# Four steps of the first batches moved in an attention-and-MoE kernel: k1's transposes, a copy of a1, the permutation of v3, the load of k4

## The chip, the core and the metric

The kernel runs on one core of one Trainium2 chip. The core has five engines with queues of their own, each worked off in order: TensorE (PE in the profile; its weight loads are PEld), VectorE (DVE), ScalarE (ACT), GpSimd (POOL) and SyncE (SP). Sixteen DMA engines serve all of them. The metric is the device time of one execution in microseconds (us). Before the change it is 252.37 us, the median of seven runs (249.28 to 253.69).

## What is computed

```python
def _attn_ref(q, k, v, p):
    def sm_attn(qq, kk, vv):
        s = scale * np.matmul(qq, kk.transpose(0, 1, 3, 2))
        s = s - np.max(s, axis=-1, keepdims=True)
        a = np.exp(s)
        a = a / (np.sum(a, axis=-1, keepdims=True) + 1e-09)
        return np.matmul(a, vv)
    p_packed = sm_attn(p, k, v)
    out = sm_attn(q, p_packed, p_packed)
    return out.astype(np.float32)

def _moe_ref(x, w_in, w_out):
    h = x @ w_in
    g = h * np.cos(h)
    return (g @ w_out).astype(np.float32)
```

q, k and v are 8 batches x 8 heads x 576 rows x 64 in float32, p is 8 x 8 x 32 x 64. In a first attention 32 packed queries per head look at all 576 keys; in the second one the 576 queries look at the 32 packed results. The heads of a row are put side by side (4608 rows of 512), go through w_in (512 x 2048), are multiplied by their own cosine, and go through w_out (2048 x 512).

## The kernel before

The kernel works batch by batch, in bf16. The loads of q, k and v (`load`) are DMAs from GpSimd's queue that cast to bf16 on the way. For each batch b there follow, by the names of the code:

- kT and qT: k and q with the head's 64 numbers on the partitions. They are made either by 24 TensorE transposes in three groups, each copied out of PSUM (`pe_T`), or by one transposing DMA on SP's queue (`xbar`).
- `s1`: scores of p against k, 16 matmuls, two exponentials on ScalarE into a1 with the sums beside them. a1T is a1 transposed, by TensorE (`a1_pe`, `a1_one`) or by a DMA on SP (`a1_xbar`).
- `permute_v`: one copy that puts v's heads side by side (vp). `pp`: 24 matmuls of vp with a1T, which give the packed results, copied to ppT.
- `ppw`: the packed results times a quarter of w_in (PPW, four quarters, n = 0 to 3). So w_in is applied to 32 packed rows per head, and the second attention is applied after it.
- `s2`, `sums2`, `normalise`: scores of q against the packed results, exponentials (a2u), their sums by a matmul with blocks of ones, a logarithm and an exponential on ScalarE for the inverse, and two products on VectorE (a2n).
- `h_mm`, once for each of 16 chunks fc of 128 hidden columns: four matmuls of PPW and a2n into a psA tile, the cosine on ScalarE, the product with the cosine on VectorE (gT).
- `out_gen`, used as `fill(n)`: the next n matmuls of gT and w_out for an earlier batch, with the copy to osb and the store on SP's queue at the end of each row block. They are spread between the other work of TensorE.

The order of the work is written out by hand; each engine runs its instructions in the order of the code. A "front" is the part from one batch's chunks to the next (table load for the exponential, `s2`, `sums2`, `normalise` and the next batch's `s1`), a "slot" (`slot`) the 16 chunks, with steps hung in after given chunks (the hooks) and fills in between. The first front, for batch 0, is lines 349 to 403 and slot 0 is lines 404 to 418; front 1 is lines 442 to 460, slot 1 lines 461 to 463, front 2 lines 465 to 499, slot 2 line 500. From batch 3 on, lines 502 to 535 repeat one pattern. `warm(n)` are matmuls on zeros in the first front.

What the change and the steps of the prediction touch:

- psA: three PSUM tiles of two banks, used in turn by nearly every step of TensorE; a chunk's tile comes free when its gT product is done. ot: two banks for the fills.
- bf: the loaded tiles. k has two buffers, q and v one each. The load of the next q waits until the transpose of the last one has read it; the load of the next v until the permutation has read it. vp has two buffers.
- GpSimd's queue holds, in the order of the code, all loads of q, k, v and the weights, the permutations of v from batch 1 on, `dup_p` for batches 2 to 7, and two joint copies per batch (line 267: the last 64 rows of gT, which two batches share).
- Lines 452 to 456 of front 1: transpose of q2 on SP, permutation of v2, load of v3, permutation of v3, load of q3. The load of k4 hangs in slot 1 after chunk 8 (line 462).
- SP's queue in fronts 1 and 2: transpose of q2 (line 452), stores, transpose of k3 (slot 1, after chunk 12), stores, transposes of q3, a1 of batch 3 and k4 (lines 483 to 486).
- Line 496: GpSimd copies one element of kT of batch 4 ("gate"), so that the loads of v4, q4 and k5 behind it are held until that transpose has landed.
- `pp(3)` is hung in slot 2 after chunk 7, `pp(4)` in slot 3 after chunk 5 (line 535).

Of the kernel before, what the change touches and what calls it, by code (L numbers as in the profile page):

```python
# [15 lines left out]
def kernel(  # L16
# [16 lines left out]
    C = 6  # L33
    TP = S // C
# [20 lines left out]
    V, ACT, G = nc.vector, nc.scalar, nc.gpsimd  # L55
# [17 lines left out]
    def copy(eng, out, in_):  # L73
        if eng is ACT:
            ACT.copy(out=out, in_=in_)  # L75
        else:
            eng.tensor_copy(out=out, in_=in_)  # L77

    def psa(dt=FP32):
        return A.tile([128, 2, 512 if dt == FP32 else 1024], dt, name="psA", tag="A")  # L80

    def load(n, b):
        bf[n, b] = bf_pool.tile([TP, H, C * D], BF16, name=n + "bf", tag=n + "bf", bufs=2 if n == "k" else 1)
        G.dma_start(out=bf[n, b], in_=srcs[n][b].rearrange("h (p c) d -> p h (c d)", c=C))

    def permute_v(b, eng=G):
        vp[b] = vp_pool.tile([TP, C, H * D], BF16, name="vp", tag="vp")
        copy(eng, vp[b].rearrange("p c (h d) -> p c h d", h=H),
             bf["v", b].rearrange("p h (c d) -> p c h d", c=C))
# [5 lines left out]
    def pe_T(n, b, engs=(V, V, V), groups=(0, 1, 2), own=False):  # L95
        if 0 in groups:
            xT[n, b] = att_pool.tile([128, H * 3, TP], BF16, name=n + "T", tag=n + "T", bufs=2 if n == "k" else 1)
        t = xT[n, b]
        flat = bf[n, b].rearrange("p h x -> p (h x)")
        for i in groups:  # L100
            ps = bank(BF16) if own else psa(BF16)[:, 0, :]
            for j in range(8):
                o = 8 * i + j
                nc.tensor.transpose(ps[:, j * TP:(j + 1) * TP], flat[:, o * 128:(o + 1) * 128],  # L104
                                    ident[0:TP, 0:TP])
            copy(engs[i], t[:, 8 * i:8 * i + 8].rearrange("p a x -> p (a x)"),
                 ps[:, 0:8 * TP])

    def bank(dt=FP32):
        return O.tile([128, 512 if dt == FP32 else 1024], dt, name="ot", tag="ot")  # L110

    def pack_p(b0, b1, flat=None):
        ng = 2 * (b1 - b0)
        if flat is None:
            flat = psa(BF16).rearrange("p a x -> p (a x)")
        for g in range(ng):
            nc.tensor.transpose(flat[:, g * 128:(g + 1) * 128],
                                p_bf[:, 2 * b0 + g].rearrange("p t d -> p (t d)"), ident)
        V.tensor_copy(out=P2[:, b0:b1].rearrange("p b h n -> p (b h n)"), in_=flat[:, 0:ng * 128])
# [14 lines left out]
    def s1(b, later=False):  # L134
        ps = scores(P2[:, b], xT["k", b])
        sm = sums1[b] = small.tile([128, 2], FP32, name="sums1")

        def exps():
            for y in range(2):
                ACT.activation(  # L140
                    out=a1[b % 2][:, y, :, 0:TP].rearrange("p (e m) x -> p e m x", e=2),
                    in_=ps[y][:, :, 0:HS].rearrange("p e (m x) -> p e m x", m=3),
                    func=AF.Exp, scale=scale, accum_out=sm[:, y:y + 1])
        if later:
            return exps
        exps()

    def recips(b):
        r1[b] = small.tile([128, 2], FP32, name="r1")
        rs1[b] = small.tile([128, 2], FP32, name="rs1")  # L150
        V.reciprocal(r1[b], sums1[b])
        V.tensor_scalar(out=rs1[b], in0=r1[b], scalar1=scale, scalar2=None, op0=ALU.mult)
# [16 lines left out]
    def a1_one(b):  # L169
        t = a1T[b] = att_pool.tile([128, 2, C, 128], BF16, name="a1T", tag="a1T")  # L170
        ps = psa(BF16)
        for y in range(2):
            for c in range(C):
                nc.tensor.transpose(ps[0:TP, y, c * 128:(c + 1) * 128], a1[b % 2][:, y, c, 0:TP], ident)
        for y in range(2):
            copy(V, t[0:TP, y].rearrange("p c x -> p (c x)"), ps[0:TP, y, 0:C * 128])

    def pp(b, own=False, engs=(V, ACT)):
        ps = bank() if own else psa()[:, 0, :]
        for hp in range(4):  # L180
            for j in range(C):
                c = 2 * (j % 3) + j // 3
                nc.tensor.matmul(ps[:, hp * 64:(hp + 1) * 64], vp[b][:, c, hp * 128:(hp + 1) * 128],  # L183
                                 a1T[b][0:TP, :, j, 32 * hp:32 * hp + 32], start=(j == 0), stop=(j == C - 1))
        pv = ps[:, 0:256].rearrange("p (a y x) -> p a y x", a=4, y=2)
        t = ppT[b % 2].rearrange("p (a y) x -> p a y x", y=2)
        for y in range(2):
            r = slice(64 * y, 64 * y + 64)
            copy(engs[0], t[r, :, y, :], pv[r, :, y, :])
        for y in range(2):  # L190
            r = slice(64 * y, 64 * y + 64)
            z = slice(64 - 64 * y, 128 - 64 * y)
            copy(engs[1], t[z, :, y, :], pv[r, :, y, :])
# [27 lines left out]
    def s2(b):  # L221
        a2u[b] = att_pool.tile([128, 2, S], BF16, name="a2u", tag="a2u")
        ps = scores(ppT[b % 2], xT["q", b])
        for y in range(2):
            ACT.activation(out=a2u[b][:, y].rearrange("p (e x) -> p e x", e=2),  # L225
                           in_=ps[y][:, :, 0:HS], func=AF.Exp, scale=rs1[b][:, y:y + 1])

    def sums2(b, y):
        if b not in lns:
            lns[b] = att_pool.tile([128, 2, S], FP32, name="lns", tag="lns")  # L230
        ps = psa()
        for e in range(2):
            nc.tensor.matmul(ps[:, e, 0:HS], ones_blk, a2u[b][:, y, e * HS:(e + 1) * HS],  # L233
                             start=True, stop=True)
        ACT.activation(out=lns[b][:, y].rearrange("p (e x) -> p e x", e=2),  # L235
                       in_=ps[:, :, 0:HS], func=AF.Ln)
# [89 lines left out]
    def fill(n):  # L326
        while n > 0 and filler[1] > 0:
            next(filler[0])
            filler[1] -= 1
            n -= 1  # L330
# [13 lines left out]
    def warm(n):  # L344
        wps = bank()
        for _ in range(n):
            nc.tensor.matmul(wps, wz[:, 0:128], wz, start=True, stop=True)  # L347
# [38 lines left out]
        load_w_out(n)  # L386
    G.dma_start(out=p_raw[:, 4:, :], in_=p_rows[:, 4:, :])
    s2(0)
    warm(3)
    sums2(0, 0)  # L390
    sums2(0, 1)
    pe_T("k", 1, (V, V, V))
    warm(2)
    s1_mm = s1(1, later=True)
    cut_ppw, rest_ppw = ppw(0, 0, V, own=True, later=True, cuts=((0, 256), (256, 512)))
    normalise(0)
    s1_mm()
    cut_ppw()
    a1_one(1)
    rest_ppw()  # L400
    load("k", 2)
    permute_v(1)
    load("v", 2)
    for fc in range(NFC):
        rest = h_mm(0, fc)
        if fc in (11, 12, 13):
            pe_T("q", 1, (V, ACT, V), (fc - 11,), own=True)
        rest()
        if fc in (1, 5, 8):
            ppw(0, 1 + fc // 4, (ACT, V), own=True)  # L410
        if fc == 3:
            recips(1)
        if fc == 10:
            pp(1, own=True, engs=(ACT, ACT))
        if fc == 13:
            set_filler(0)
        if fc >= 14:
            fill(2)

    def slot(s, hooks, keep=0, heavy={}):  # L420
        left = filler[1] - keep
        out_eng[:] = (ACT,) if s > 1 else (V, ACT)
        weight = [1 + heavy.get(fc, 0) for fc in range(NFC)]
        for fc in range(NFC):
            h_mm(s, fc)()
            quota = (left * sum(weight[:fc + 1])) // sum(weight) - (left + keep - filler[1])
            first = quota
            while hooks and hooks[0][0] == fc:
                if first == quota and fc in heavy:
                    first = quota // 2  # L430
                    fill(first)
                hooks.pop(0)[1]()
            fill(quota - first if first != quota else quota)

    def pw2(b, n=0, eng=None):
        ppw(b, n, eng)
        ppw(b, n + 1, eng)

    def tk(n, b, i):
        return lambda: pe_T(n, b, (V, V, V), (i,))  # L440
# [11 lines left out]
    xbar("q", 2)  # L452
    permute_v(2)
    load("v", 3)
    permute_v(3)
    load("q", 3)
    ppw(1, 1, V)
    normalise(1)
    ACT.preload_act_table_set(SIN_SET)
    fill(14)  # L460
    slot(1, [(3, lambda: pw2(1, 2, (ACT, V))), (5, tk("k", 2, 0)), (6, tk("k", 2, 1)),
             (7, tk("k", 2, 2)), (8, lambda: load("k", 4)), (9, lambda: pack_p(2, 5)),
             (11, lambda: pack_p(5, B)), (12, lambda: xbar("k", 3))], 4, {3: 3})

    ACT.preload_act_table_set(EXP_SET)
# [1 line left out]
    fill(1000)  # L467
    set_filler(1)
    s1(2)
    fill(5)  # L470
    a1_pe(2, (0,))
    fill(2)
# [24 lines left out]
    for n, b in (("v", 4), ("q", 4), ("k", 5)):  # L497
        load(n, b)
    fill(5)
    slot(2, [(7, lambda: pp(3, engs=(ACT, ACT))), (11, lambda: pw2(3))], 5, {11: 3})  # L500

    for s in range(3, B):
        nxt = s + 1 < B
# [66 lines left out]
```

## Time and profile before

| what | us |
|---|---|
| median of seven runs | 252.37 |
| the runs | 249.28 to 253.69 |
| the profiled execution's own time | 252.37 |
| its span, first to last instruction | 250.6 |
| TensorE matmul busy | 236.3 |
| VectorE / ScalarE / GpSimd busy | 167.3 / 167.0 / 57.4 |
| granted TensorE clock, mean | 0.999 |

The stretches of the first part, as busy microseconds of each engine and as the rate of the DMA engines:

| stretch (us) | PE | DVE | ACT | POOL | GB/s |
|---|---|---|---|---|---|
| 10 to 20 | 8.65 | 5.40 | 5.82 | 3.85 | 205 |
| 20 to 25 | 3.94 | 4.73 | 4.38 | 1.47 | 205 |
| 25 to 30 | 4.49 | 4.97 | 4.45 | 2.07 | 206 |
| 30 to 35 | 4.24 | 4.54 | 4.12 | 3.88 | 206 |
| 35 to 40 | 5.00 | 4.35 | 4.85 | 0.82 | 206 |
| 50 to 60 | 9.77 | 8.71 | 5.54 | 3.52 | 145 |
| 60 to 70 | 9.92 | 6.97 | 5.56 | 4.22 | 229 |
| 70 to 80 | 9.60 | 7.79 | 6.74 | 1.18 | 169 |
| 80 to 90 | 9.29 | 6.82 | 7.84 | 0.18 | 166 |
| 110 to 120 | 8.36 | 6.48 | 7.08 | 2.99 | 143 |

How to read the lines that follow. A line of the timeline has a start, a length, the engine, the line of the kernel, the operation, the tile that it writes, the tile that it reads, the shape and the count; square brackets give the idle time of the engine just ahead of it and what ended that. The chain of waits goes from what ended last back to what released it; it is shown in order of time, with a start and a length. A line of the waits names who waited, for what, the sum in us, how often and the longest. "To landing" is the time from a DMA's issue until its data had arrived.

### The profile page before, as it was taken

The page shows a single profiled execution, that of the slowest core. Times are in us where ns is not written, and L with a number is a line of the kernel's source. Part 1 is how long each engine was busy: PE and PEld are TensorE (multiplying, and loading weights), DVE is VectorE, ACT ScalarE, POOL GpSimd, SP SyncE. Part 2 cuts the span into 40 slices and gives each one's busy share as a digit, 9 for nine tenths or more (in the row PEclk, how much of TensorE's full clock was granted, in tenths as well). Part 3 has the DMA queues.
Part 4 walks back from the last instruction along what each step waited for, and adds up shares of the span by engine and source line. Part 5 has one row for each costly group of instructions (what it writes and reads, how often), then busy time and mean ns, then how long its engine had stood idle before and what let it go on. Part 6 is the DMA issues. An engine that isn't in the chain of part 4 may idle for free.

```text
span 250.6 us, 5070 instructions
## 1 busy us (share of the span) xinstructions
PE 236.3 (94%) x2038; PEld 131.3 (52%) x2038; DVE 167.3 (67%) x253; ACT 167.0 (67%) x278; POOL 57.4 (23%) x68
## 2 busy tenths in 40 slices
PE   8688899999999899979999999999999999999993
PEld 3454474566544554455546654565456554665452
DVE  2449997689668767676848666678766774876110
ACT  2358899746566787868867867887777684874000
POOL 8162543250430043103330405020500000000000
PEclk9999999999999999999999999999999999999999
DMA  6999999999999989996999996989391112202133
GB/s 90 202 205 205 205 206 228 199 163 137 239 175 166 179 148 214 155 190 131 193 195 220 161 220 141 186 160 207 80 167 42 42 44 67 61 15 66 44 86 84
DMA packets 63175, 37.09 MB, mean 148 GB/s; under 512 B 35792, under 2 KB 58576, under 8 KB 63152
## 3 DMA queue, kind: packets, MB, share of 16 engines
q0 software_dynamic: 23152, 18.75, 49.7%
q1 hardware_dynamic: 39840, 17.90, 35.6%
q8 instruction: 16, 0.26, 0.5%
q10 hardware_dynamic: 160, 0.13, 0.2%
q14 instruction: 7, 0.06, 0.1%
HBM read 37.22 MB, written 9.44 MB: 186 GB/s over the span
## 4 chain that ended last, share of the span: by engine, by line
PE 72%; DMA 17%; DVE 5%; ACT 2%; POOL 2%; issue 1%; DVEq 0%; POOLq 0%
PE ot L309 43%; PE psA L256 19%; DMA w_out_bf<-in_moe_w_out_dram 9%; DMA w_in_bf<-in_moe_w_in_dram 7%; DVE gT L263 3%; PE psA L207 3%; PE psA L183 2%; DMA a1T<-a 2%; PE psA L129 2%; ACT cosT L260 2%; PE ot L295 1%; PE psA L233 1%; DVE PPW L77 1%; ACT ppT L75 1%; DVE a2n L243 1%
## 5 line engine op out<-in xcount | busy, mean ns | idle before, releaser
L309 PE MATMUL ot<-w_out_bf,gT 128*128 128x512 bf16 x512 | 133.3, 379 | 0.1
L263 DVE TENSOR_TENSOR gT<-psA,cosT 128x576 bf16<-128x576 f32 x128 | 93.8, 756 | 28.9 <-ACT cosT L260 28.1
L260 ACT ACTIVATE cosT<-psA 128x576 bf16<-128x576 f32 x128 | 82.5, 652 | 27.8 <-PE psA L256 23.1
L256 PE MATMUL psA<-a2n,PPW 128*128 128x288 bf16 x512 | 83.5, 286 | 1.4 <-DVE PPW L77 0.4
L309 PEld LDWEIGHTS <-gT 128*128 128x128 bf16 x512 | 47.7, 98 | 43.3 <-issue 6.8
L256 PEld LDWEIGHTS <-PPW 128*128 128x128 bf16 x512 | 49.3, 98 | 34.5 <-issue 4.2
L77 DVE CAST PPW<-psA 128x1024 bf16<-128x1024 f32 (+1 forms) x23 | 26.9, 1175 | 11.6 <-PE psA L207 11.5
L77 DVE COPY osb<-ot 128x512 f32<-128x512 f32 (+1 forms) x24 | 16.3, 679 | 17.5 <-PE ot L309 13.9
L267 POOL COPY joint<-gT 128x512 bf16<-128x512 bf16 x16 | 9.9, 617 | 78.9 <-DVE gT L263 78.9
L77 POOL COPY vp<-vbf 96x3072 bf16<-96x3072 bf16 x7 | 19.3, 2751 | 14.3 <-DMA vbf<-in_v_dram 14.3
L75 ACT COPY osb<-ot 128x512 f32<-128x512 f32 (+1 forms) x13 | 7.3, 565 | 15.3 <-PE ot L309 10.6
L243 DVE SCALAR_TENSOR_TENSOR a2n<-a2u,r,lns 128x576 bf16<-128x576 bf16 x16 | 12.3, 813 | 7.3 <-ACT lns L241 7.3
L235 ACT ACTIVATE lns<-psA 128x576 f32<-128x576 f32 x16 | 10.2, 650 | 7.1 <-PE psA L233 6.5
L140 ACT ACTIVATE a<-psA 128x576 bf16<-128x576 f32 x16 | 10.3, 647 | 6.7 <-PE psA L129 6.7
L309 PE MATMUL ot<-w_out_bf,joint 128*128 128x512 bf16 x48 | 12.8, 379 | 0.0
L75 ACT CAST ppT<-psA 64x128 bf16<-64x128 f32 x24 | 6.2, 260 | 9.1 <-DVE ppT L77 6.0
L225 ACT ACTIVATE a2u<-psA,rs 128x576 bf16<-128x576 f32 x16 | 11.0, 737 | 1.4 <-PE psA L129 1.3
L207 PE MATMUL psA<-w_in_bf,ppT 64*32 64x512 bf16 x224 | 10.2, 381 | 0.0
L241 ACT ACTIVATE lns<-lns 128x576 f32<-128x576 f32 x16 | 10.0, 676 | 0.0
L347 PE MATMUL ot<-wz 128*128 128x512 bf16 x26 | 8.1, 447 | 1.2 <-DVE wz L359 1.2
L522 POOL COPY gate<-kT 1x1 bf16<-1x1 bf16 x3 | 0.5, 181 | 36.6 <-DMA kT<-kbf 36.6
L77 DVE COPY kT<-psA 128x768 bf16<-128x768 bf16 x8 | 4.2, 552 | 6.8 <-PE psA L104 6.6
(71 smaller groups left out, 155.9 us busy)
## 6 DMA issues: line engine op xcount, KB each, us to landing
kbf<-in_k_dram POOLq DMA_DIRECT2D x8, 576.0 KB, 12.9
vbf<-in_v_dram POOLq DMA_DIRECT2D x8, 576.0 KB, 8.6
qbf<-in_q_dram POOLq DMA_DIRECT2D x8, 576.0 KB, 10.1
out_dram<-osb SPq DMA_DIRECT2D x24, 192.0 KB, 3.1
out_dram<-osb SPq DMA_DIRECT2D x22, 128.0 KB, 2.4
w_in_bf<-in_moe_w_in_dram POOLq DMA_DIRECT2D x4, 512.0 KB, 17.1
w_out_bf<-in_moe_w_out_dram POOLq DMA_DIRECT2D x4, 512.0 KB, 21.4
out_dram<-osb SPq DMA_DIRECT2D x26, 64.0 KB, 2.1
```

What stands on the lines that cost most here:

```text
L75: ACT.copy(out=out, in_=in_)
L77: eng.tensor_copy(out=out, in_=in_)
L140: ACT.activation(out=a1[b % 2][:, y, :, 0:TP].rearrange("p (e m) x -> p e m x", e=2), in_=ps[y][:, :, 0:HS].rearrange("p e (m x) -> p e m ...
L207: nc.tensor.matmul(ps[y][32 * x:32 * x + 32, :], ppT[b % 2][r, 2 * x + y, :], w_in_bf[r, x, n * 512:(n + 1) * 512], start=True, stop=True)
L225: ACT.activation(out=a2u[b][:, y].rearrange("p (e x) -> p e x", e=2), in_=ps[y][:, :, 0:HS], func=AF.Exp, scale=rs1[b][:, y:y + 1])
L235: ACT.activation(out=lns[b][:, y].rearrange("p (e x) -> p e x", e=2), in_=ps[:, :, 0:HS], func=AF.Ln)
L241: ACT.activation(out=lns[b][:, y], in_=lns[b][:, y], func=AF.Exp, scale=-1.0)
L243: V.scalar_tensor_tensor(out=a2n[b][:, y], in0=a2u[b][:, y], scalar=r1[b][:, y:y + 1], in1=lns[b][:, y], op0=ALU.mult, op1=ALU.mult)
L256: nc.tensor.matmul(ps[:, e, 0:HS], PPW[b][:, y, fc * 128:(fc + 1) * 128], a2n[b][:, y, e * HS:(e + 1) * HS], start=(y == 0), stop=(y == 1))
L260: ACT.activation(out=csv, in_=ps[:, :, 0:HS], func=AF.Sin, bias=PI_HALF)
L263: V.tensor_tensor(out=gT[b][:, fc, :].rearrange("p (e x) -> p e x", e=2), in0=ps[:, :, 0:HS], in1=csv, op=ALU.mult)
L309: nc.tensor.matmul(pss[c], w, w_out_bf[:, fc, :], start=(fc == 0), stop=(fc == NFC - 1))
```

## The change

Four edits, all in the part up to slot 2:

1. In the first front the three groups of k1's transposes, which stood behind both sums of batch 0, are put ahead of, between and behind the two sums. The warm-up matmuls around them go from 3 and 2 to 1 and 3.
2. `a1_one(1)` copies the first half of a1T of batch 1 on VectorE as before and hands back the second copy, which ScalarE makes after chunk 0 of slot 0. The call moves behind `rest_ppw()`.
3. The permutation of v3 moves from GpSimd in front 1 to VectorE in slot 2, after chunk 4.
4. The load of k4 moves from slot 1 (after chunk 8) to front 2, behind `s1(2)`.

```diff
@@ a1_one @@
-        for y in range(2):
-            copy(V, t[0:TP, y].rearrange("p c x -> p (c x)"), ps[0:TP, y, 0:C * 128])
+        copies = [lambda eng, y=y: copy(eng, t[0:TP, y].rearrange("p c x -> p (c x)"), ps[0:TP, y, 0:C * 128])
+                  for y in range(2)]
+        copies[0](V)
+        return copies[1]
@@ first front @@
     s2(0)
+    warm(1)
+    for i in range(3):
+        pe_T("k", 1, (V, V, V), (i,))
+        if i < 2:
+            sums2(0, i)
     warm(3)
-    sums2(0, 0)
-    sums2(0, 1)
-    pe_T("k", 1, (V, V, V))
-    warm(2)
     s1_mm = s1(1, later=True)
...
     cut_ppw()
-    a1_one(1)
     rest_ppw()
+    rest_a1 = a1_one(1)
     load("k", 2)
@@ slot 0 @@
         rest()
+        if fc == 0:
+            rest_a1(ACT)
@@ front 1 and slot 1 @@
     load("v", 3)
-    permute_v(3)
     load("q", 3)
...
-             (7, tk("k", 2, 2)), (8, lambda: load("k", 4)), (9, lambda: pack_p(2, 5)),
+             (7, tk("k", 2, 2)), (9, lambda: pack_p(2, 5)),
@@ front 2 @@
     s1(2)
+    load("k", 4)
@@ slot 2 @@
-    slot(2, [(7, lambda: pp(3, engs=(ACT, ACT))), (11, lambda: pw2(3))], 5, {11: 3})
+    slot(2, [(4, lambda: permute_v(3, V)), (7, lambda: pp(3, engs=(ACT, ACT))), (11, lambda: pw2(3))], 5, {11: 3})
```

## The prediction

> **What bounds the kernel now.** I read the page's busy times first, then its chain of work that ended last, then TensorE's waits, and last the timelines of the four places that the edits touch.
>
> ```profile
> span 250.6 us, 5070 instructions
> PE 236.3 (94%) x2038; PEld 131.3 (52%) x2038; DVE 167.3 (67%) x253; ACT 167.0 (67%) x278; POOL 57.4 (23%) x68
> ```
>
> TensorE (PE) is idle for only 14.3 us of the span, so a reordering that leaves its work alone can win no more than part of that. The chain of waits says where the first stretch stands:
>
> ```profile
> 5.10 0.76 POOL w_in_bf L333
> 5.85 16.43 DMA w_in_bf<-in_moe_w_in_dram
> 22.57 21.75 DMA w_out_bf<-in_moe_w_out_dram
> 44.36 0.81 PE ot L309 x3
> ```
>
> Up to 44 us the end is set by loads that run back to back. The table of stretches gives 205 GB/s from 10 to 25 us and 206 from 25 to 40, so the stream has no hole to close. TensorE meets it three times: at the fourth projection in slot 0 (w_in's last quarter, 31.08 us), at the transposes of q1 (34.01), and at the first fill that needs w_out's last quarter (44.36). From 35 to 45 us it is busy 9.88 of 10 us. What TensorE waits for after that is in its own waits:
>
> ```profile
> PE psA L183 <- DVE gT L263: 1.6, 1, 1.6
> PE psA L183 <- DMA a1T<-a: 0.7, 1, 0.7
> PE ot L207 <- DMA w_in_bf<-in_moe_w_in_dram: 0.5, 1, 0.5
> ```
>
> The 0.7 is `pp(3)` in slot 2 (86.33 us), which waits for a1T of batch 3: transpose issued at 81.62, landed 4.57 later, at 86.19. The 1.6 is `pp(4)` in slot 3 (111.99 us). It is put down to a gT product that ended at 111.91, but `pp` takes the psA tile of two chunks further back, free by then. Its other input is a1T of batch 4, issued at 107.91; the tile's view gives 3.9 us to landing: 111.8. I take both stalls as transposes that came late. That they are late follows from the DMA queue:
>
> ```profile
> 55.05 4.07 SPq L93 DMA_TRANSPOSE qT<-qbf  x1
> 62.86 5.47 SPq L93 DMA_TRANSPOSE kT<-kbf  x1
> 65.78 2.75 POOL L77 COPY vp<-vbf 96x3072 bf16<-96x3072 bf16 x1 [9.85 <-DMA vbf<-in_v_dram]
> 68.47 0.77 POOL L84 DMA_DIRECT2D qbf<-in_q_dram  x1
> 69.79 0.77 POOL L84 DMA_DIRECT2D kbf<-in_k_dram  x1
> 72.16 0.15 PEld L129 LDWEIGHTS <-P 64*32 64x32 bf16 x16 [0.42 <-DMA kT<-kbf]
> 78.18 3.35 SPq L93 DMA_TRANSPOSE qT<-qbf  x1
> 81.62 3.11 SPq L156 DMA_TRANSPOSE a1T<-a  x1
> ```
>
> Read it upwards: a1T(3) follows qT(3) on SP, qT(3) waited 6.3 us for q3, and q3's load stood behind the permutation of v3 on POOL, until 68.47.
>
> **The change part by part.** *k1's transposes between the sums.* The 24 transposes (1.40 us of PE) stay and move ahead of the sums; the warm-up matmuls fall from five to four. Better: k1's copies (three of 0.50 on VectorE) run while ScalarE still does the exponentials (16.88 to 18.25). Worse: the second sum now stands behind the second group, whose psA tile comes free only after the second exponential, so its logarithm and the inverse behind it start up to 0.6 later. I take 0, bounds -0.5 and +0.6, local to the front.
>
> *Second a1 copy to ScalarE.* VectorE loses one copy of 0.51 (1.02 for two, 22.96 us). The rest of the first projection's eviction no longer stands behind the a1 copies; the second projection, which waits 0.46 for it at 24.36, can start earlier. ScalarE gains one copy; the nearest row is its 128x768 copy of qT, 0.80. It is queued ahead of chunk 1's cosine, and behind that stand chunk 1's product, the eviction of the second projection and chunks 4 to 7. In 25 to 30 us VectorE is busy 4.97 of 5 and ScalarE 4.45, so load goes to the freer one; chunk 4 (waits today for that eviction) moves by -0.9 to +0.5. The cover of both edits is the 0.51 us that TensorE waits for w_in at 31.08, then q1 and w_out; the sum after 44 us is 0. Without that cover the two would cost up to 1.1.
>
> *v3 permuted by VectorE in slot 2.* POOL loses 2.75 us. VectorE gains one copy; the row is its permutation of v0 at 11.27 us, same shape, 0.96. It is queued after the product of chunk 4; behind it on VectorE stand the products of chunks 5 to 7, and `pp(3)` takes the psA tile of chunk 5.
>
> ```profile
> 83.20 2.98 DVE L263 TENSOR_TENSOR gT<-psA,cosT 128x576 bf16<-128x576 f32 x4 [0.27 <-ACT cosT L260]
> ```
>
> These four are chunks 3 to 6, back to back, 0.745 each: chunk 4 ends at 84.69, chunk 5 at 85.43. With 0.96 between them chunk 5 ends at 86.39, and `pp(3)` starts 0.08 later, at 86.47 against 86.33 now. So even if a1T(3) comes earlier, the stall of 0.7 is only handed over: +0.1. Bounds: -0.7 where VectorE has caught up, +0.3 if it has not. The slot of v3's tile is now free only at about 85.7; v4's load waits for its gate until 89.78 anyway.
>
> *q3 and k4 loaded earlier.* With the permutation gone from POOL, q3's load waits only for its one buffer, which the transpose of q2 frees: 55.05 plus 11.3 to landing is 66.35. So q3 goes out at about 66.5, 2.0 earlier. k4, now issued in front 2 and behind the two joint copies of 0.62, goes out at about 68.5 against 69.79, 1.3 earlier. This has two ends.
>
> The gain: qT(3), a1T(3), kT(4), the gate and the loads of v4, q4, k5 all hang on q3 and can come up to 2.0 earlier, and with them a1T(4), now 1.56 late for TensorE. That takes away 0 to 1.56.
>
> The price: kT(3), which the scores at 72.16 need. It landed at 62.86 plus 9.0 = 71.86, and TensorE's fills ahead of the scores ended at 72.22, so there is some 0.3 of slack.
>
> ```profile
> 68.00:70.00 2.00, 2.00 (x32) 1.28 (x30) 1.10 (x4) 0.29 (x2) 2.00 (x4) 1.00 1.28 298
> 70.00:72.00 2.00, 2.00 (x32) 0.66 (x29) 1.58 (x2) 1.45 (x3) 1.18 (x2) 1.00 0.75 94
> ```
>
> The last column is GB/s. The transpose of k3 has the engines to itself at 298 (its packets run from 67.5 to 69.9 in the DMA records); then q3 starts slowly at 94. Moved 2.0 earlier, q3 comes in at about 68.2 and is up to speed at 70, over the last 0.8 to 1.7 of the transpose's 2.4 us. What sharing costs is in the same queue: the transpose of q2, beside the loads of k3 and v3, took 11.3 to land, against 5.2 for the quickest transpose of a q: 6.1 for a whole one. A third of one (0.8 of 2.4) is 2.0, seven tenths 4.3, all of it 6.1; nothing, if q3 starts as slowly as today. I take the third, since the slow start is the nearest row: 2.0 less the slack of 0.3 is +1.7; bounds 0 and +4.0.
>
> On this sharing the Trainium skill ("DMA: Bandwidth & Descriptors", Queues, rings and completion order) says that each DMA engine takes turns between its queues, packet by packet. By even turns the last 0.8 would take 1.6, a price of 0.5 after the slack, and the whole sum would be -1.0 in place of +0.2; the trace's 11.3 against 5.2 is more than a doubling, so I go by the row.
>
> *Sum*, on the profiled run (252.37 = span 250.6 + 1.8 around it; also the median of the seven runs): front 0, scores of batch 3 +1.7, `pp(3)` +0.1. At `pp(4)` TensorE then arrives 1.8 later than now, after an a1T that is no later than now: -1.56. Together +0.2: **252.6**.
>
> **The rivals.** *Full collision (slower).* q3's packets start so early that most of kT(3) runs in shared time. TensorE's queue is in order: fills, exponentials and the normalisation of batch 2 all stand behind the scores of batch 3. Price 4.0 to 5.8, plus 0.1, less 1.56: +2.5 to +4.3, 254.9 to 256.7. For it: q2's transpose shows the whole price. Against it: the load's slow start. It decides from a kT(3) landing after about 76.
>
> *No collision (faster).* kT(3) is through before q3 counts; the earlier q3 takes away all of `pp(4)`'s stall, perhaps `pp(3)`'s too: -1.5 to -2.3, 250.1 to 250.9. For it: only 2.0 us of shift against a start that takes over 1.5. Against it: VectorE's permutation stands where the first stall was.
>
> *Nothing arrives.* q3 comes earlier but finishes as late as now, since it then shares with kT(3): the old stalls stay, less what TensorE is later; 252.4 to 252.9. It lies inside my forecast's range.
>
> **How the numbers follow.** Forecast, partial collision: 0.50, its own range 251.3 to 254.5 (price 0.4 to 3.6). Full collision 0.26, no collision 0.18, nothing arrives 0.06. The range over the cases, cut to leave two in ten outside, is 250.6 to 255.9. A change under 1%, 2.5 us, can hardly be told from none here (the seven runs span 249.28 to 253.69). All stalls that this change can reach add to 2.3 us, so faster by over 1% needs luck: 0.10. Slower by over 1% is the full collision and the upper edge of the forecast: 0.28. Within 1%: 0.62.
>
> **What would show it.** In the changed profile: q3's load at about 66.5 with no permutation ahead of it; the landing of kT(3) near 74 in place of 71.86, and a TensorE wait of 1 to 3 us at the scores of batch 3 (line 129); a 0.96 permutation on VectorE near 85, and `pp(3)` put down to gT; no wait over 0.5 at `pp(4)`; the first fill on w_out's last quarter still near 44.4. I am wrong if that fill moves, if kT(3) lands as before, or if VectorE's permutation stalls TensorE by more than 0.5 beyond today.

## The result, and the profile after

The changed kernel takes 255.02 us, the median of 27 runs (250.5 to 260.06). The kernel before, run beside it, takes 251.27 (64 runs, 249.27 to 255.81). The ratio is 1.0104, with a 95% interval of 1.007 to 1.0137: slower by about one per cent. This ratio leaves out runs more than 1.5% above a kernel's fastest (18 of the 27 here, 26 of the 64 of before), and what the change does makes many of its runs long, so the medians over all runs (3.75 us apart) stand beside the ratios below.

The profiled execution of the changed kernel took 258.23 us, 5.9 more than that of before, with a span of 256.5 in place of 250.6. It lies in the upper part of the runs: it shows where time goes, at more than its typical size. First the page: the span, the busy times, and the clock that TensorE was granted, in tenths, over 40 slices.

```profile
span 256.5 us, 5069 instructions
PE 239.0 (93%) x2037; PEld 132.3 (52%) x2037; DVE 167.5 (65%) x253; ACT 167.4 (65%) x279; POOL 54.6 (21%) x67
PEclk9999999999986999999999999999999999999999
```

TensorE is busy 2.7 us more on the same work (less one warm-up matmul), and its clock has a dip (8, 6) between 70.5 and 83.3 us that the kernel before has not. Next, TensorE's waits in the changed kernel: for whom, the sum, how often, the longest.

```profile
PE psA L129 <- DMA kT<-kbf: 5.8, 1, 5.8
...
PE psA L185 <- DVE gT L265: 0.6, 1, 0.6
```

The 5.8 is new: the scores of batch 3 wait for the transpose of k3. The 0.6 stands where `pp(3)` waited 0.7 for a1T; it is now put down to VectorE's product, as predicted. The 1.6 at `pp(4)` is gone. The chain of waits now runs through that transpose (start, length):

```profile
63.59 14.12 DMA kT<-kbf
77.71 0.04 issue
77.75 0.68 PE psA L129 x12
```

It was issued 0.7 later than before (63.59 against 62.86) and took 14.1 to land in place of 9.0. The timeline of the same stretch, on SP, POOL, PE and DVE:

```profile
54.81 5.12 SPq L93 DMA_TRANSPOSE qT<-qbf  x1
63.59 7.72 SPq L93 DMA_TRANSPOSE kT<-kbf  x1
68.93 0.77 POOL L84 DMA_DIRECT2D qbf<-in_q_dram  x1 [13.24 <-DMA qT<-qbf]
70.81 0.77 POOL L84 DMA_DIRECT2D kbf<-in_k_dram  x1
77.75 0.68 PE L129 MATMUL psA<-kT,P 64*32 64x288 bf16 x16 [5.83 <-DMA kT<-kbf]
78.79 2.31 PE L311 MATMUL ot<-w_out_bf,gT 128*128 128x512 bf16 x5
92.16 0.95 DVE L77 COPY vp<-vbf 96x3072 bf16<-96x3072 bf16 x1
117.83 0.86 PE L185 MATMUL psA<-a1T,vp 96*128 96x64 bf16 x24
```

Two things are to be seen. q3's load is no longer behind a permutation: it waits for the transpose of q2 alone. But that transpose landed only at 68.3 in this execution (13.5 after its issue, 11.3 before), so q3 went out at 68.93, no earlier than the 68.47 of before. v3 was late too (issued at 54.92, 15.3 to landing, 70.2). Behind the permutation q3 would have gone out some 3 us after that, as it does, at 73.32, in the kernel below with all but the v3 edit. And the five fills behind the scores took 2.31 us, where the same five took 1.25 before. The windows of two microseconds say why: the columns are busy time of PE, PEld, DVE, ACT, POOL, then the clock, the DMA engines' busy share and GB/s.

```profile
72.00:74.00 2.00, 0.00 (x0) 0.00 (x0) 0.04 (x1) 0.00 (x0) 0.00 (x0) 1.00 1.34 80
74.00:76.00 2.00, 0.00 (x0) 0.00 (x0) 0.00 (x0) 0.00 (x0) 0.00 (x0) 0.80 1.51 161
76.00:78.00 2.00, 0.24 (x16) 0.18 (x24) 0.00 (x0) 0.00 (x0) 0.00 (x0) 0.50 1.25 248
78.00:80.00 2.00, 2.00 (x27) 0.58 (x12) 1.06 (x1) 1.37 (x4) 0.00 (x0) 0.50 1.23 272
80.00:82.00 2.00, 2.00 (x8) 1.05 (x7) 0.40 (x3) 0.37 (x1) 0.00 (x0) 0.50 1.30 207
82.00:84.00 2.00, 2.00 (x24) 0.65 (x23) 0.82 (x1) 1.98 (x5) 0.00 (x0) 0.99 1.21 270
```

TensorE stands still from 72 on; from 75 or so its clock is halved, and it stays at 0.50 for some four microseconds after the work is back. The Trainium skill ("TensorE: Matmul & The Clock Gate", Part 1) says that a gap of about 3.4 us without work lets the clock fall to half; the rows agree, with the fall some 3 us into the standstill.

The 5.9 us follow from start times in both traces. The scores of batch 3 start at 77.75 against 72.16: +5.6. The first chunk of batch 2 starts at 86.31 against 78.68: +7.6, so 2.0 more, and of these the doubled scores (0.24), fills (1.06) and sums (0.52) at half clock make 1.8. `pp(3)` starts at 93.83 against 86.33: +7.5. `pp(4)` starts at 117.83 against 111.99: +5.8. From there to the end it stays +5.9.

### The profile page after: what moved, and what is told of

It is laid out like the page before. It is cut to its first block, busy times and chain, and to the rows that moved or that the text cites. A ratio compares the mean times of both kernels' runs of the same rounds, so it can differ in the third digit from the quotient of the medians.

```text
span 256.5 us, 5069 instructions
## 1 busy us (share of the span) xinstructions
PE 239.0 (93%) x2037; PEld 132.3 (52%) x2037; DVE 167.5 (65%) x253; ACT 167.4 (65%) x279; POOL 54.6 (21%) x67
## 4 chain that ended last, share of the span: by engine, by line
PE 70%; DMA 15%; DVE 7%; ACT 3%; POOL 2%; issue 2%; SPq 0%; DVEq 0%; POOLq 0%
PE ot L311 42%; PE psA L258 18%; DMA vbf<-in_v_dram 10%; DMA kT<-kbf 6%; DVE gT L265 4%; PE psA L209 3%; ACT cosT L262 2%; PE psA L129 2%; PE psA L235 2%; PE psA L185 1%; PE ot L297 1%; POOL vp L77 1%; DVE PPW L77 1%; DVE vp L77 1%; ACT ppT L75 1%
## 5 line engine op out<-in xcount | busy, mean ns | idle before, releaser
L140 ACT ACTIVATE a<-psA 128x576 bf16<-128x576 f32 x16 | 10.2, 646 | 12.3 <-PE psA L129 12.3
L75 ACT COPY osb<-ot 128x512 f32<-128x512 f32 (+1 forms) x13 | 7.3, 565 | 15.3 <-PE ot L311 10.6
L77 POOL COPY vp<-vbf 96x3072 bf16<-96x3072 bf16 x6 | 16.5, 2752 | 3.6 <-DMA vbf<-in_v_dram 3.6
L349 PE MATMUL ot<-wz 128*128 128x512 bf16 x25 | 9.2, 510 | 1.2 <-DVE wz L361 1.2
L129 PE MATMUL psA<-kT,P 64*32 64x288 bf16 x128 | 4.2, 305 | 6.1 <-DMA kT<-kbf 5.8
L84 POOL DMA_DIRECT2D qbf<-in_q_dram x8 | 6.2, 776 | 15.4 <-DMA qT<-qbf 13.2
```

The source lines that it names most:

```text
L140: ACT.activation(out=a1[b % 2][:, y, :, 0:TP].rearrange("p (e m) x -> p e m x", e=2), in_=ps[y][:, :, 0:HS].rearrange("p e (m x) -> p e m ...
```

## The experiments

My theory: the permutation that GpSimd did in front 1 was a gate. It held q3's and k4's loads until v3 had landed, plus 2.75 us; without it these loads fall into the transpose of k3. The rivals: one of the other edits makes the loss; VectorE's copy makes it; or the transpose is late for a reason that q3 and k4 have no part in. The kernels of a group below ran on the same chip, beside the same runs of the kernel before; each group ran on another chip, so times are compared within a group and ratios between groups.

### One part alone, one part undone, the gate put back

`e1_v3_only` is the kernel before with nothing but the third edit:

```diff
     load("v", 3)
-    permute_v(3)
     load("q", 3)
@@ slot 2 @@
-    slot(2, [(7, lambda: pp(3, engs=(ACT, ACT))), (11, lambda: pw2(3))], 5, {11: 3})
+    slot(2, [(4, lambda: permute_v(3, V)), (7, lambda: pp(3, engs=(ACT, ACT))), (11, lambda: pw2(3))], 5, {11: 3})
```

> The kernel before with the third edit alone: v3 permuted by VectorE in slot 2, so that q3's load no longer stands behind the permutation on GpSimd. Theory 'lost gate' (GpSimd's permutation kept q3's load out until v3 had landed and k3's transpose had the DMA engines to itself; without it k3's transpose lands late and TensorE waits at the scores of batch 3): all of the change's loss is here, 253.5 to 256.5 us, with a wait of 2 to 6 us at line 129. Theory 'VectorE' (the 0.96 us copy in slot 2 stalls the chunks): also slow, 253 to 255, but the wait stands in slot 2 and none at line 129. Theory 'front' (k1's transposes or the a1 copy cost): as before, 250.5 to 252.

`e2_undo_v3` is the changed kernel with these lines the other way round (permutation back on GpSimd, the other three edits kept):

> The changed kernel with the third edit undone; the front and the place of k4's load stay changed. Lost gate and VectorE: back at the kernel before, 250.3 to 252.3 us, k3's transpose landing before 73. Front: still 253.5 to 256.

`e3_both_permutes` is the changed kernel with `permute_v(3)` put back in front 1 as well, so that the gate stands and VectorE copies too:

> The changed kernel with v3 permuted twice: by GpSimd in front 1 as before the change (its result is not used) and by VectorE in slot 2. The work on VectorE is that of the change, q3's load is held as before it. Lost gate: 250.3 to 252.5 us, within 0.5 of the run with the edit undone. VectorE: 253.5 to 256, as the changed kernel.

`e4_k3_early` is the changed kernel with the transpose of k3 right behind that of q2 on SP, ahead of the stores of slot 1:

```diff
     xbar("q", 2)
+    xbar("k", 3)
@@ slot 1 @@
-             (11, lambda: pack_p(5, B)), (12, lambda: xbar("k", 3))], 4, {3: 3})
+             (11, lambda: pack_p(5, B))], 4, {3: 3})
```

> The changed kernel with k3's transpose issued right behind q2's in front 1 instead of after chunk 12 of slot 1, so that it is through before q3's load can start. Lost gate: no wait above 0.5 us at the scores of batch 3, 249 to 251.5 us, at or below the kernel before. VectorE or front: no gain, 253.5 to 256. It can fail in its own way if both transposes now share with v3's load and land after 73.

| kernel | median (range, runs) | ratio to before (251.29) | wait at the scores of batch 3 |
|---|---|---|---|
| v3 edit alone | 256.02 (253.88 to 259.7, 6) | 1.018 (1.0108 to 1.0251) | 6.4 |
| all but the v3 edit | 251.14 (249.17 to 254.09, 12) | 0.997 (0.9922 to 1.0018) | none |
| changed, both permutations | 253.55 (249.92 to 254.86, 12) | 1.0053 (1.0007 to 1.01) | none |
| changed, k3's transpose early | 254.13 (250.53 to 257.37, 12) | 1.0045 (0.9992 to 1.0097) | none |

TensorE's waits in the kernel with the v3 edit alone:

```profile
PE psA L129 <- DMA kT<-kbf: 6.4, 1, 6.4
```

One edit carries the whole loss, and the other three together are worth nothing that can be measured. The third and fourth kernel have lost the wait, but not all of the time: both lie above what was expected of them (250.3 to 252.5, and 249 to 251.5). Their profiles show another stall, early, among the chunks of slot 0. This is the timeline of the kernel with both permutations:

```profile
28.49 3.21 DVE L152 TENSOR_SCALAR rs<-r 128x2 f32<-128x2 f32 x1
28.91 2.76 POOL L77 COPY vp<-vbf 96x3072 bf16<-96x3072 bf16 x1
32.41 1.84 PE L258 MATMUL psA<-a2n,PPW 128*128 128x288 bf16 x7 [3.05 <-DVE gT L265]
```

A product of 128 x 2 numbers on VectorE (`recips(1)`, line 152) usually takes 0.17 us. Here it lasted 3.21 and ended when GpSimd's copy ended; TensorE waited 3.05 for the product behind it. The kernel with all but the v3 edit shows the same at 30.15 us, 2.11 long; as that kernel stands at 0.997, the held product alone is not shown to make the difference. The kernel before has the same two operations close together (and a product of 0.48 at 68.08 us beside the permutation of v3), so this could also be what spreads its runs.

### Moving the small product away

The next four kernels move `recips(1)` so that it can't meet GpSimd's copy:

```diff
-        if fc == 3:
+        if fc == 12:
             recips(1)
```

`f1_before_recips_late` is the kernel before with this:

> The kernel before with the two small reciprocals of batch 1 behind chunk 12 of slot 0 instead of chunk 3, where GpSimd's permutation of v1 can't run beside them. Theory 'port' (the scattered times of the kernel before, near 250 and near 254 us, come from the 128x2 product on VectorE that is held for up to 3.2 us when GpSimd has begun its load issue and permutation first): the upper group goes, all runs 249 to 251.8, median near 250.2, ratio 0.994 or less. Rival 'DMA' (the upper group comes from late transposes): the spread stays, 249.3 to 255, median near 251.3.

`f2_after_recips_late` is the changed kernel with it:

> The changed kernel with the same move of the reciprocals. Lost gate: without the other stall what is left is the late transpose of k3 alone, 251 to 258 us, median 253.5 to 257, a wait of 1 to 6 us at the scores of batch 3, and 3 us or more above the kernel before with this move. Port alone (the change only makes the held product more likely): as the kernel before with this move, 249 to 251.8.

`f3_after_recips_k3early` has the early transpose of k3 in addition:

> The changed kernel with the reciprocals moved and k3's transpose issued behind q2's. Both theories together: neither stall is left, 249 to 251.5 us, median 250 to 250.8, no wait above 0.5 at the scores of batch 3. If the copy of v3 on VectorE or the shared time of the two transposes costs on its own, 251.5 to 254.

`f6_undo_v3_recips` is the changed kernel without the v3 edit, with it:

> The changed kernel with the permutation of v3 back on GpSimd in front 1 and the reciprocals moved; the front and the place of k4's load stay changed. Lost gate and port: 249 to 251.8 us, within 0.4 of the kernel before with the reciprocals moved, which prices the front's two edits and k4's place at nothing. If those edits cost or gain by themselves, the difference shows it here without the scatter.

| kernel | median (range, runs) | ratio to before (250.65) | wait at the scores of batch 3 |
|---|---|---|---|
| before, product late | 251.15 (249.9 to 255.64, 12) | 1.0016 (0.9993 to 1.004) | none |
| changed, product late | 254.01 (252.42 to 257.04, 6) | 1.0141 (1.0102 to 1.0181) | 5.2 |
| the same, k3's transpose early | 252.08 (249.86 to 258.49, 12) | 1.003 (1.0002 to 1.0057) | 1.2 |
| all but the v3 edit, product late | 249.99 (249.34 to 255.48, 12) | 0.9982 (0.9956 to 1.0009) | none |

The first is a miss: 3 of 12 runs still lie above 253.7 (6 of 29 of the kernel before do), so the held product is not all that spreads the runs. In the changed kernel the wait and the loss stay, so they have nothing to do with the held product. With the transpose of k3 moved early most of the wait goes, but not the time: the profile shows a new wait of 2.0 for an eviction (line 209), presumably because the stores behind the transpose on SP are held, which no run isolated. The kernel missed its 249 to 251.5 with that. TensorE's waits in that kernel:

```profile
PE psA L209 <- DVE PPW L77: 2.0, 1, 2.0
...
PE psA L129 <- DMA kT<-kbf: 1.2, 1, 1.2
```

The fourth kernel was expected within 0.4 us of the first, and lies 1.2 below it by the medians. By the ratios it is 0.34% (0.9 us) below, and the intervals overlap: that the front's edits and k4's place gain up to some 1 us is neither shown nor excluded.

### Another gate, and half a gate

The sharpest question is whether it is q3's and k4's loads, and which. `f5_after_recips_gated` keeps the permutation on VectorE and holds both loads by a copy of one element of kT of batch 3:

```diff
     load("v", 3)
-    load("q", 3)
@@ front 2 @@
     s1(2)
+    G.tensor_copy(out=gate, in_=xT["k", 3][0:1, 0, 0:1])
+    load("q", 3)
     load("k", 4)
```

> The changed kernel with the inverse of the sums of batch 1 (recips(1)) after chunk 12, and with the loads of q3 and k4 held on GpSimd by a one-element copy of kT of batch 3, so that neither load goes out before that transpose has landed. Theory (the removed permutation was an accidental gate, and any gate in its place restores it): kT(3) lands by 73, no TensorE wait at line 129, 249.5 to 251.5 where the kernel before stands at 250.7; perhaps a new stall of up to 2 us at pp(3), since q3 is later and a1 of batch 3 stands behind it on SP. Rival (the transpose is slow because of v3's tail, the stores or something else ahead of it, not because of q3 and k4): kT(3) still lands after 75, a wait of 3 to 6 us at line 129, 253 to 256.

`g2_gate_k4_only` leaves `load("q", 3)` where the change has it and holds k4 alone by the same copy:

> The changed kernel with recips(1) after chunk 12; q3's load goes out freely, only k4's is held by a one-element copy of kT of batch 3. If q3's load alone makes kT(3) late: a wait of 3 to 6 us at line 129 as without any gate, a ratio to the kernel before of 1.010 to 1.016. If it takes both loads, or k4's: the wait falls below 1.5, ratio 0.998 to 1.005.

`g1_both_permutes_recips` has both permutations and the late product:

> The changed kernel with GpSimd's permutation of v3 put back (so the gate stands) beside VectorE's, which writes the same numbers once more, and recips(1) after chunk 12. Against the same kernel without VectorE's copy it prices that copy alone. Theory: the 0.96 copy in slot 2 is worth 0 to 0.5 us, since pp(3) waited 0.7 there already: 250.0 to 250.6, a ratio to the kernel before of 0.998 to 1.002. Rival: VectorE is full in slot 2 and the copy costs all of its 0.96 or more: 251 to 251.7, 1.002 to 1.006.

`f7_after_recips_warm` fills TensorE's standstill with zeros:

```diff
     fill(5)
+    warm(24)
     s1(3)
```

> The changed kernel with recips(1) after chunk 12 and 24 matmuls on zeros (0.21 us each at full clock, 5.1 in all) ahead of the scores of batch 3, where TensorE stood still for 5 us. Theory: the clock falls to half after the standstill and costs 1 to 1.5 us behind it; with the zeros it stays at 1.00 from 72 to 84 us and the kernel takes 252.5 to 253.2, against 254.0 without them (ratio 1.007 to 1.011). Rival: only the landing of kT(3) counts, and the slow stretch is made up at later waits: 253.7 to 254.5, ratio 1.012 to 1.016; where kT(3) lands early the zeros are a loss of up to 5.

| kernel | median (range, runs) | ratio to before (251.18) | wait at the scores of batch 3 |
|---|---|---|---|
| both loads gated | 251.11 (249.77 to 254.05, 12) | 1.0015 (0.9982 to 1.0048) | 0.4 |
| k4 alone gated | 256.26 (251.39 to 261.21, 12) | 1.0073 (1.0032 to 1.0114) | 7.1 |
| both permutations | 251.12 (249.92 to 253.65, 12) | 1.001 (0.9977 to 1.0043) | none |
| zeros in the standstill | 256.07 (254.91 to 259.86, 6) | 1.0205 (1.0158 to 1.0251) | 3.0 |

GpSimd's queue in the kernel with both loads gated, from its timeline:

```profile
72.60 0.18 POOL L473 COPY gate<-kT 1x1 bf16<-1x1 bf16 x1 [7.20 <-DMA kT<-kbf]
73.14 0.77 POOL L84 DMA_DIRECT2D qbf<-in_q_dram  x1 [0.36 <-issue]
```

and in the kernel with k4 alone gated:

```profile
68.06 0.77 POOL L84 DMA_DIRECT2D qbf<-in_q_dram  x1 [13.24 <-DMA qT<-qbf]
...
78.34 0.18 POOL L474 COPY gate<-kT 1x1 bf16<-1x1 bf16 x1 [8.35 <-DMA kT<-kbf]
78.89 0.77 POOL L84 DMA_DIRECT2D kbf<-in_k_dram  x1 [0.36 <-PE psA L129]
```

The two kernels differ only in where q3's load stands, and their medians lie 5.2 us apart: seven of twelve runs with q3 free lie above 256, none with q3 held above 254.1. (The ratio with q3 free is 1.0073, below the 1.010 to 1.016 that I expected, and its interval overlaps that of the other kernel.) With q3 held to 73.14, the transpose landed at 72.6 (10.1 after its issue); with q3 let go at 68.06 it landed at 78.3 (16.2), though k4 was not even issued by then. So letting q3's load go out is the cause, and k4's load isn't needed for it. The gate has its own price: q3 comes so late that `pp(3)` waits 1.9 us for a1T of batch 3 (issued at 83.90, 3.9 to landing, 87.8). This is from TensorE's waits in the kernel with both loads gated:

```profile
PE psA L185 <- DVE gT L265: 1.9, 1, 1.9
```

The kernel with both permutations prices VectorE's copy. Its wait at `pp(3)` is 0.6, and its ratio of 1.001 stands against 0.9982 for the same kernel without the copy, on another chip. That is 0.3%, give or take 0.4, so a copy that costs nothing and one that costs 0.7% both fit. The ratio is that of the theory and the median of 251.12 lies in the rival's range: the run does not decide between them.

The zeros missed. Their 5.34 us were not enough, since the transpose took 16.1 to land in that execution; TensorE still stood still for 3.05, and the clock fell to 0.50 all the same: a standstill of 3.05 us was enough, and the fall came 2.4 us into it, at 79.4. It takes no single wait of 3 us either: in the kernel with k3's transpose early and the product late, waits of 1.24 and 1.96 with scores of 0.44 between them (72.3 to 75.9) were followed by a clock of 0.50 from 76.9 to 80.3. Where the transpose is quicker the zeros can only cost: the fastest run is 254.91, against 252.42 without them on another chip. So the price of the clock is read from the trace above (1.8 in that execution) and was not isolated by a run.

### How the load delays the transpose

My prediction put the price down to shared bandwidth. The landings, in us from issue, and the packets of k3's transpose (2304 of 256 bytes) in the DMA records say more. The table has every profiled kernel but the two that issue k3's transpose earlier:

| profiled kernel | q3's load | v3 | q2's transpose | k3's transpose | its dense packets end | from there to landing |
|---|---|---|---|---|---|---|
| before, product late | behind the permutation | 11.0 | 11.8 | 8.6 | 70.0 | 2.1 |
| before | same | 10.6 | 11.3 | 9.0 | 69.75 | 2.1 |
| all but the v3 edit, product late | same | 11.4 | 11.7 | 9.6 | 69.5 | 2.0 |
| both permutations, product late | same | 11.9 | 12.3 | 9.9 | 72.25 | 0.5 |
| both loads gated | behind the gate | 12.3 | 11.5 | 10.1 | 72.0 | 0.6 |
| both permutations | behind the permutation | 14.3 | 14.1 | 10.9 | 72.5 | 2.2 |
| all but the v3 edit | same | 15.5 | 13.3 | 11.4 | 73.0 | 2.1 |
| changed, product late | free | 15.0 | 14.0 | 13.0 | 74.25 | 2.8 |
| changed | free | 15.3 | 13.5 | 14.1 | 74.25 | 3.5 |
| v3 edit alone | free | 15.4 | 13.3 | 15.6 | 73.75 | 4.4 |
| zeros in the standstill | free | 17.3 | 15.2 | 16.1 | 75.5 | 4.6 |
| k4 alone gated | free | 15.7 | 13.6 | 16.2 | 73.5 | 4.8 |

With q3 free, the time from the last dense packets to landing runs beside q3's packets and is 2.8 to 4.8 us in place of 0.5 to 2.2. That is nearly all that the two share. q3's packets (768 bytes) begin in numbers only 4.8 to 5.3 us after the issue where the load is free, 1.5 to 2.8 after it where it was held: in the changed kernel the first is at 73.86, when some 2100 of the transpose's 2304 had gone. Against the kernel before, this end makes 1.4 of the 5.1 us by which the transpose is longer. Whether q3's packets make it longer is not shown: they run beside it in the kernel with both permutations too (from 73.55), and there it takes 2.2.

The rest are stops, two in each kernel with q3 free. In the changed kernel the packets run from 68.75 to 69.5, stop until 71.0, run, stop again from 72.0 to 73.5, and end; in the stops next to nothing moves (GB/s in the last column):

```profile
69.50:71.00 1.50, 1.50 (x30) 0.56 (x28) 0.88 (x2) 0.93 (x3) 1.50 (x4) 1.00 0.14 33
72.00:73.50 1.50, 0.00 (x0) 0.00 (x0) 0.04 (x1) 0.00 (x0) 0.00 (x0) 1.00 1.38 13
```

q3's packets are in neither of them. The first stop stands in all rows with v3 at 14 and more, gated or not: the last of v3's shares is still on its way at 69 to 70 (71 in the kernel with the zeros), and the packets of k3's transpose stop until one to two microseconds after it. The second stands in two gated rows as well. In the kernel with both loads gated it lasts from 70.25 to 71.5, after v3 had landed (67.9) and before q3 was issued (73.14):

```profile
70.30:71.50 1.20, 1.04 (x27) 0.56 (x28) 0.84 (x2) 0.76 (x2) 0.00 (x0) 1.00 0.05 6
```

No gated row has both stops, every free one has. At like lateness of v3 (14.3 to 15.7) the transpose takes 10.9 to 11.4 behind a gate and 13.0 to 16.2 without one.

What stays open is how letting q3 go brings about the rest. v3 and q2's transpose are late in every profile with q3 free, though q3's load is issued after them, and only in two of seven with the gate. In this table they are late in just those executions that took 254 us and more, and all profiles with q3 free are of that kind: a quick run of the changed kernel (its fastest took 250.5) was not profiled, so that lateness may go with long executions and not with q3. Nor is the second stop explained. It begins some 0.5 us after a 16 KB packet of the instruction queue starts (at 71.54 in the changed kernel, at 69.80 with both loads gated), in all seven rows that have it; before, that packet came at 69.66, as k3's last packets went. No run moved it. And the share of runs in which the transpose is quick although q3 is free was not measured.

## Why the prediction was half right

*The time.* 252.6 was predicted, 255.02 measured, inside the range of 250.6 to 255.9. But the likeliest case was "partial collision", up to 254.5, and the case that came was the rival that I gave 0.26, the full collision with 254.9 to 256.7: kT(3) landed at 77.7, beyond the 76 from which I said that it decides. Only its time and its wait came, though. That rival had "most of kT(3) in shared time", and q3's packets began when some 2100 of the transpose's 2304 had gone. That the range holds the result owes more to its width than to the mechanism.

*The place* was right: the loss sits where the q3 load meets the transpose of k3, at the scores of batch 3. The v3 edit alone brings it (1.018), without it it is gone (0.997), and gating the loads undoes it (1.0015).

*The step that failed* is the price of kT(3), "+1.7; bounds 0 and +4.0". In the profiled execution it was 5.6, and 2.0 more from the slow stretch behind it. The working failed in two ways. I timed the collision from q2's transpose landing as in the old trace (66.35, so "q3 goes out at about 66.5"), but in this execution it landed at 68.3 and q3 went out at 68.93. And the price stood on an overlap, q3's packets over "the last 0.8 to 1.7 of the transpose's 2.4 us", paid for in shared bandwidth. That overlap is not in the records. The transpose is 5.1 longer: 3.1 are the two stops, about 0.5 a later first packet, and only the 1.4 at its end lie beside q3's packets. The 11.3 against 5.2 that I took for the price of sharing gives 5.8 for the whole transpose, near the measured 5.6; with no overlap to go with it, that is luck.

*What was not foreseen* is the clock: a wait of this length is not paid once, it makes the work behind it slower. My full collision of "4.0 to 5.8" had no term for it, and it was worth 1.8 here.

*pp(3)* was right: the 0.95 copy on VectorE took over the place of a1T, the wait stayed at 0.6 where it had been 0.7, predicted +0.1 and measured -0.1. *pp(4)*: -1.56 predicted, -1.7 measured. But the reason is TensorE's own lateness, which I named, and not an earlier q3: it wasn't earlier.

*The front edits* were worth nothing that could be measured, as predicted, and in part for the reason given. In the changed kernel TensorE waits 0.8 for ScalarE's copy of a1T (24.73 us), and the wait for w_in's last quarter shrinks from 0.5 to 0.2. From 35 to 45 us it is busy 9.96 of 10 us, 9.88 before. The cover does not take up all of it: the first chunk behind the fills on w_out's last quarter starts at 44.71 against 45.00, 0.3 earlier. *k4's place* costs nothing that can be measured, as the gate for k4 alone and the kernels without the v3 edit show.

*The rival "no collision"* is refuted for the typical run, and a kernel that beats both was not found: all but the v3 edit, with the product late, stands at 0.9982 with an interval that takes in 1.

## What to carry to other kernels

An instruction that is taken off an in-order queue may have been holding back what stands behind it: before moving it, ask which DMA it held, and whose transfer is on the way when that DMA goes out. If a slow transpose is near the critical path, keep the gate (one element copied from its result is enough, at 0.18 us), but count what the held load feeds. And price a TensorE wait of some 3 us or more, or two of 1.2 and 2.0 close together as in one kernel here, higher than its length.

## What the runs showed of the hardware

A copy of 96 x 3072 bf16 on GpSimd can hold a tiny VectorE operation until it ends: 2.11 and 3.21 us in place of 0.17. The Trainium skill ("GPSIMD Engine Reference", Key points) says that GpSimd shares its SBUF interfaces with VectorE, and that they contend when the VectorE instruction has two SBUF inputs or runs in a 2-port mode. The shared interfaces agree with the hold; in which mode the product ran, no run shows. VectorE's own permutation of the same tile takes 0.95, GpSimd's 2.75.

A transpose by DMA whose packets begin while the last of a load's shares are still on their way doesn't just share with them: its packets stop for 0.9 to 2.3 us, nearly all at once (seven profiles), and little other data flows meanwhile (33 GB/s from 69.5 to 71 us in the changed kernel, against 298 in the transpose's free run before). A second stop, of 1.25 to 1.5 us, comes without any load on the way (6 GB/s in the kernel with both loads gated).
